# Performer attention and GEGLU on one core: one weighting of v moved to VectorE, and the stage between two tiles in another order

## The chip, the cores and the metric

The kernel runs on one core of one Trainium2 chip. The metric is the device time of one execution in microseconds (us). Most executions of one kernel agree within some tenths of a per cent: the 95% intervals of the ratios below reach 0.12 to 0.25% to each side, those of the three slow experiments (e10, e11, e13) up to 0.36%.

## The reference, cut to what matters

```python
q, k, v: (8 batches, 8 heads, 576, 64);  omega: (128, 64)
phi(x) = exp(x omega^T - |x|^2/2 - max) / sqrt(128)      # q and k scaled by 64^-1/4 first
kv  = phi(k)^T v ;  z = sum of phi(k)
num = phi(q) kv  ;  den = phi(q) z ;  attn = num / den
x   = attn as 4608 tokens x 512
out = (gelu(x w_gate) * (x w_val)) w_out                 # 512 -> 1536 -> 512
```

## The kernel before

The kernel interleaves the attention of one batch with the feed-forward of a tile of 512 tokens. It does not let a scheduler choose: every engine runs its instructions in the order in which the Python calls record them. So "an order" is a list of calls, and a change of order is a permutation of that list. The calls that the change and the argument touch:

```python
def fill(n):                    # n matmuls on zeros, results not used: work to keep TensorE going
    fill_ps = mo_tile([P, P], F32, "fill_ps")
    for _ in range(n):
        nc.tensor.matmul(fill_ps, still[:, :P], still[:, :P])

def load_v(b, eng=nc.gpsimd):   # 1152 KB, float32
    t = ld.tile([P, HP, R * D], F32, name="vf")
    loads.append(eng.dma_start(out=t, in_=rows_of(v, b)))

class Attention:                # a, n, m, o are batches 0, 1, 2, 3
    def by_dma(self, nm): ...   # k or q transposed by DMA, issued on SyncE's queue
    def kf(self, c, ...): ...   # TensorE: pk <- omegaT, kT
    def kx(self, c): ...        # ScalarE: k_p <- exp(pk)
    def km(self, c): ...        # VectorE: nmax <- max(pk)
    def qf / qx / w: ...        # pq; q_pT <- exp(pq); ScalarE: wk <- exp(nmax)
    def v(self, half, eng):     # v_ext <- v * wk, one half of the columns, 128x1152
        eng.tensor_mul(vev[:, isl, :, :D], vfv[:, isl], wkv[:, isl]...)
        eng.tensor_copy(vev[:, isl, :, D], wkv[:, isl])
    def kz / kzc: ...           # 72 matmuls of k_p with v_ext; copy of the result
    def nd / nx: ...            # q_pT with kz; x_sb <- num / den on VectorE
    def xd(self, i): ...        # nc.sync.dma_start_transpose: xT <- x_sb
    def xt / xc: ...            # the same by TensorE and a copy

    # feed-forward of a tile
    def ts(self, n, eng):       # x sum number n of four: difference of two parts of xT, 128x512
        eng.tensor_sub(t[:, n], p, q)       # two SBUF inputs; sum 1 reads sum 0
    def vm / vs / va: ...       # x w_val with 7 products in place of 8, out of w_val and the x sums
    def ga / gp / ge: ...       # x w_gate and gelu
```

In names, `val_one` and `val_two` are the products of `vm`, `g_ps` the gate, `o_ps` the projection of the tile before.

The softmax here doesn't subtract the row's maximum and nothing guards it: scores larger than these inputs give would overflow.

Of the kernel before, what the change touches and what calls it, by code (L numbers as in the profile page):

```python
# [15 lines left out]
def kernel(  # L16
# [11 lines left out]
    nc = tc.nc  # L28
# [40 lines left out]
    def mo_tile(shape, dtype, name):  # L69
        return mo.tile(shape, dtype, name=name, tag="mo")  # L70


    def rows_of(src, b):
        return src[b].rearrange("(j e) (p r) d -> (e p) j (r d)", e=2, r=R)
# [3 lines left out]
    def load_kq(nm, b, parts=1):  # L78
        src = {"k": k, "q": q}[nm]
        t = ld.tile([P, NI, P], BF16, name=f"{nm}_in")  # L80
        tv = t.rearrange("p i x -> p (i x)").rearrange("p (j y) -> p j y", j=HP)
        n = HP // parts
        loaded[nm, b] = t
        loads.extend(nc.gpsimd.dma_start(out=tv[:, c * n:(c + 1) * n],
                                         in_=rows_of(src, b)[:, c * n:(c + 1) * n])
                     for c in range(parts))
        return loads[-parts:]

    def load_v(b, eng=nc.gpsimd):
        t = ld.tile([P, HP, R * D], F32, name="vf")  # L90
        loaded["v", b] = t
        loads.append(eng.dma_start(out=t, in_=rows_of(v, b)))
        return loads[-1:]
# [37 lines left out]
    def fill(n):  # L131
# [3 lines that stand above are left out]
# [19 lines left out]
    act, dve, pool = nc.scalar.copy, nc.vector.tensor_copy, nc.gpsimd  # L154
# [425 lines left out]
    def after(dmas):  # L580

        behind(last["begun"], dmas)

    def behind(one, dmas):
        for dma in dmas:
            tc.add_manual_dep(dma.ins, one.ins.name, mybir.DependencyInfo(
                mybir.DependencyClass.Sync, mybir.DependencyReason.DATA))
# [5 lines left out]
    def first():  # L593
# [9 lines left out]
        a = Attention(0)  # L603
# [41 lines left out]
        a.qt.pe(0)  # L645
        fill(12)
        a.qf(1, True)
        a.v(1, pool)
        a.qt.copy(0, dve)
        a.v(0, nc.vector)  # L650
        fill(12)
# [6 lines left out]
        n = Attention(1)  # L658
# [4 lines left out]
        h = Gated(1)  # L663
# [112 lines left out]
        p = Projection(0, g)  # L776
# [3 lines left out]
        n.kx(1)  # L780
        n.km(1)
        m = Attention(2)
        behind(loads[-2], [m.by_dma("k")])
        m.by_dma("q")
        n.kt.pe(3)
# [20 lines left out]
        p.mm(0, 11, 12)  # L806
        n.km(2)
        n.w()
        p.oc(0, act)
        p.st(0)  # L810
        p.mm(2, 0, 3)
# [3 lines left out]
        m.kf(1, False)  # L815
        m.kx(1)
        p.mm(2, 6, 9)
        p.mm(3, 0, 3)
        m.kf(0, False)
        n.v(0, nc.vector)  # L820
        n.kz(0, True)
        m.km(1)
        m.qf(0, False)
        m.qx(0)
        m.km(0)
        n.v(1, pool)
        n.kz(1)
        m.kx(0)
        p.mm(3, 3, 6)
        p.mm(3, 6, 7)  # L830
        load_v(2, nc.sync)
        n.kzc(dve)
        n.nd(0, False)
        m.qf(1, True)
        m.qx(1)
        n.nd(1, False)
        p.mm(2, 9, 10)
        n.nx(0)
        n.nx(1)
        p.mm(2, 10, 12)  # L840
        n.xd(0)
        n.nd(2, False)
        p.oc(2, act)
        fill(12)
        n.nd(3, True)
        m.qf(2, False)
        n.xd(1)
        n.nx(2)
        n.xd(2)
        n.nx(3)  # L850
        m.kf(2, False)
        m.km(2)
        fill(12)
        n.xt(3)
        n.xc(3, dve)
        m.kf(3, True)
        m.km(3)
        m.qx(2)
        h.ts(0, nc.gpsimd)
        m.tails(False)  # L860
        m.qx(4)
        m.km(4)
        p.mm(3, 7, 10)
        h.ga(0, 0)
        m.kx(2)
        p.mm(3, 10, 12)
        o = Attention(3)
        n.nd(4, False)
        m.kx(3)
        m.w()  # L870
        p.oc(3, act)
        n.nx(4)
        h.ga(0, 1)
        after(load_kq("k", 3) + load_kq("q", 3) + load_v(3))
        m.qf(3, True)
        h.ts(2, nc.vector)
        m.qx(3)
        h.vm(0, 1)
        h.vs(0, 1, act)
        m.kx(4)  # L880
        h.vm(0, 5)
        h.ts(1, nc.vector)
        m.v(1, nc.vector)
        m.v(0, nc.vector)
        h.ga(6, 0)
        h.vm(0, 6)
        h.ga(6, 1)
        h.ts(3, nc.vector)
        h.vs(0, 6, act)
        p.st(3)  # L890
        h.vs(0, 5, act)
        h.vm(0, 7)
        h.va(0, 2)
        h.vm(0, 2)
        h.gp(7, 0, 2)
        h.gp(7, 2, 4)
        h.vm(0, 3)
        h.va(0, 1)
        h.vm(0, 4)
        h.va(0, 0)  # L900
        h.ge(6)
        m.kz(0, False)
        m.kz(1)
        m.kzc(dve)
        h.vm(1, 1)
        h.vm(1, 5)
        h.vm(1, 2)
        h.vs(1, 1, act)
        h.high(0, 0, nc.vector)
        h.ge(0)  # L910
        m.nd(0, False)
        h.vs(1, 5, dve)
        h.ge(7)
        h.vm(1, 6)
        h.vs(1, 6, act)
        p.st(2)
        h.high(0, 1, nc.vector)
        h.gp(1, 0, 2)
        h.gp(1, 2, 3)
        h.gp(1, 3, 4)  # L920
        h.ge(1)
        n.xd(4)
        m.nx(0)
        m.xd(0)
        h.vm(1, 3)
        h.vm(1, 7)
        h.va(1, 0)
        h.va(1, 1)
        h.va(1, 2)
        h.gp(2, 0, 2)  # L930
        m.nd(1, False)
        m.nx(1)
        h.low(1, nc.gpsimd)
        h.low(0, nc.gpsimd)
        h.vm(2, 1)
        h.vm(2, 5)
        h.vs(2, 1, act)
        o.by_dma("k")
        m.xd(1)
        h.vs(2, 5, dve)  # L940
        h.gp(3, 0, 2)
        h.vm(2, 6)
        h.high(1, 1, nc.gpsimd)
        h.gp(2, 2, 3)
        h.vs(2, 6, act)
        h.vm(1, 4)
        h.high(1, 0, nc.vector)
        h.gp(2, 3, 4)
        h.vm(2, 2)
        h.ge(2)  # L950
        o.by_dma("q")
        h.vm(2, 7)
        h.va(2, 2)
        h.vm(2, 3)
        h.va(2, 1)
        m.nd(2, False)
        m.nx(2)
        h.va(2, 0)
        h.gp(8, 0, 2)
        h.gp(8, 2, 4)  # L960
        h.ge(8)
        h.vm(2, 4)
        h.vm(3, 1)
        h.vs(3, 1, dve)
        h.gp(3, 2, 3)
        h.vm(3, 5)
        m.nd(3, False)
        h.vs(3, 5, act)
        h.low(2, nc.vector)
        h.high(2, 0, nc.vector)  # L970
        h.gp(5, 0, 2)
        p.st(1)
        h.vm(3, 6)
        h.gp(3, 3, 4)
        h.vm(3, 3)
        m.nx(3)
        h.vs(3, 6, act)
        h.vm(3, 2)
        h.va(3, 0)
        h.vm(3, 7)  # L980
        h.va(3, 2)
        h.ge(3)
        h.va(3, 1)
        h.gp(9, 0, 2)
        h.gp(9, 2, 4)
        h.ge(9)
        h.high(3, 1, nc.gpsimd)
        m.nd(4, False)
        h.high(2, 1, nc.gpsimd)
        h.vm(4, 1)  # L990
        h.vm(4, 5)
        h.vm(4, 2)
        h.vs(4, 1, act)
        m.xd(2)
        m.nx(4)
        h.vm(3, 4)
        h.high(3, 0, nc.vector)
        h.vm(4, 6)
        h.gp(4, 0, 2)
        h.gp(4, 2, 3)  # L1000
        h.gp(4, 3, 4)
        h.vs(4, 6, act)
        h.vm(4, 7)
        h.ge(4)
        h.vs(4, 5, dve)
        h.vm(4, 3)
        h.va(4, 2)
        h.low(3, nc.gpsimd)
        h.vm(5, 1)
        h.vs(5, 1, act)  # L1010
        h.va(4, 1)
        h.vm(5, 5)
        h.vs(5, 5, act)
        h.gp(10, 0, 2)
        h.gp(10, 2, 4)
        h.va(4, 0)
        h.vm(5, 2)
        h.va(5, 0)
        h.ge(10)
        h.high(4, 1, nc.gpsimd)  # L1020
        h.vm(5, 6)
        h.low(4, nc.gpsimd)
        h.vm(4, 4)
        h.high(4, 0, nc.vector)
        h.gp(5, 2, 3)
        h.gp(5, 3, 4)
        h.vm(5, 3)
        h.vs(5, 6, act)
        h.vm(5, 7)
        h.va(5, 2)  # L1030
        h.gp(11, 0, 2)
        h.gp(11, 2, 4)
        h.va(5, 1)
        h.ge(5)
        h.ge(11)
        h.low(5, nc.vector)
        h.vm(5, 4)
        m.xd(3)
        h.high(5, 0, nc.vector)
        h.high(5, 1, nc.vector)  # L1040
        m.xd(4)
        return h, o
    def step(t, p, a, n):
# [453 lines left out]
    with tc.manual_schedule(engines={E.Activation, E.PE, E.DVE, E.SP, E.Pool}):  # L1497
        g, a = first()
        for t in range(2, N_TOK):
            p = Projection(t - 1, g)  # L1500
            if t + 1 < B:
                n = Attention(t + 2) if t + 2 < B else None
                g, a = step(t, p, a, n), n
            else:
                g = bare(t, p)
        end(Projection(N_TOK - 1, g))
# [30 lines left out]
```

## Time and profile before

| | before |
|---|---|
| time | 341.71 us (3 runs, 341.54 to 342.11) |
| span of the profiled run | 340.1 us, granted clock 0.996 |
| wk of batch 0 begins | 14.89 us |
| first nd of batch 0 | 20.34 us |
| first pk of batch 2 | 55.10 us |
| first nd of batch 2 | 74.71 us |
| first pk of the next tile's stage | 91.04 us |

In the lines of the profile PE is TensorE, PEld its weight loads, DVE is VectorE, ACT ScalarE, POOL GpSimd, SPq the queue on which SyncE issues transfers, and L134 is line 134 of the kernel. A line of a timeline gives the start in us, the length in us, engine, line, operation, out<-in with their sizes, the count, and in brackets how long the engine stood idle before and what ended that.

The prediction below shows most of the lines of this profile. One group it does not show turned out to decide the case. It is GpSimd's product of v with wk, and GpSimd's x sums, of the whole kernel before; the three numbers are minimum, median and maximum in ns, then come the first and the last start:

```profile
L271 POOL TENSOR_TENSOR v_ext<-vf,wk x12: 2145/2155/3322, 15.2 to 244.6; 128x1152 bf16<-128x1152 f32 x12
L455 POOL TENSOR_TENSOR x_sums<-xT,x_sums x10: 1142/1148/1154, 97.7 to 238.2; 128x512 bf16<-128x512 bf16 x10
```

The same product takes 2.15 us or 3.32 us on the same engine. The long ones are those at 15.20 and 54.50, where VectorE multiplies the other half of v at the same time.

### The profile page before, as it was taken

To read this page: it belongs to the slowest core of one execution; us is meant where nothing else is said; L and a number is where in the kernel's file an instruction comes from. 1 tells how busy PE (TensorE), PEld (TensorE's weight loads), DVE (VectorE), ACT (ScalarE), POOL (GpSimd) and SP (SyncE) were. 2 spreads that over 40 slices of the span, in tenths; PEclk is the share of its full clock that TensorE was granted. 3 is DMA by queue.
4 is the path that set the end of the run, shared out by engine and by line. 5 is a ranking of instruction groups with operands and counts; after the bars stand their busy time and mean duration, and the time that the engine had idled before them with its cause. 6 is when DMAs were issued, how large, how long until landed. Compare 5 with 4: busy or idle time off the path is not lost.

```text
span 340.1 us, 7996 instructions
## 1 busy us (share of the span) xinstructions
PE 328.1 (96%) x3118; PEld 206.9 (61%) x3159; DVE 229.5 (67%) x483; ACT 214.3 (63%) x434; POOL 149.5 (44%) x152
## 2 busy tenths in 40 slices
PE   8889999999999999999999999999999999999994
PEld 4566455666646664566447654665466786686683
DVE  2975389989773768375936674667457677796783
ACT  3895366774778558756875677658765446626650
POOL 8326014123496447744684559477968400000000
PEclk9999999999999999999999999999999999999998
DMA  8999999699999255945497529871413040014004
GB/s 161 276 206 207 206 265 177 155 163 221 196 144 328 53 102 87 328 92 108 58 319 120 112 28 287 170 106 33 94 33 62 10 104 22 1 28 97 2 0 124
DMA packets 66437, 44.95 MB, mean 132 GB/s; under 512 B 46688, under 2 KB 59232, under 8 KB 66400
## 3 DMA queue, kind: packets, MB, share of 16 engines
q0 software_dynamic: 14848, 22.12, 31.7%
q1 hardware_dynamic: 51088, 21.51, 31.0%
q10 hardware_dynamic: 464, 0.82, 0.7%
q8 instruction: 24, 0.39, 0.5%
q14 instruction: 13, 0.11, 0.1%
HBM read 37.78 MB, written 9.44 MB: 139 GB/s over the span
## 4 chain that ended last, share of the span: by engine, by line
PE 84%; DVE 7%; issue 2%; ACT 2%; DMA 2%; POOL 1%; SPq 0%; DVEq 0%
PE g_ps L433 20%; PE o_ps L559 18%; PE val_one L378 11%; PE val_two L378 9%; PE out_one L533 5%; PE out_two L533 3%; PE g_ps L425 3%; PE v_ps L462 3%; PE kz_ps L285 3%; PE pk L220 2%; PE nd L302 2%; DVE nmax L233 2%; PE pq L242 2%; DVE x_sb L314 2%; DVE val_c L387 1%
## 5 line engine op out<-in xcount | busy, mean ns | idle before, releaser
L433 PE MATMUL g_ps<-xT,w_gate_sb 128*128 128x512 bf16 x352 | 108.2, 379 | 0.5
L440 ACT ACTIVATE g_gelu<-g_ps 128x512 bf16<-128x512 f32 x108 | 63.6, 597 | 54.1 <-PE g_ps L433 26.5
L559 PE MATMUL o_ps<-w_out_sb,gated 128*128 128x512 bf16 x275 | 64.6, 380 | 1.1 <-issue 0.6
L480 POOL TENSOR_TENSOR gated<-g_gelu,val_c 128x512 bf16<-128x512 bf16 x29 | 33.7, 1162 | 53.1 <-DVE iden L313 26.7
L387 DVE TENSOR_TENSOR val_c<-val_one,val_c 128x256 f32<-128x256 f32 x48 | 20.4, 424 | 49.0 <-ACT g_gelu L440 40.0
L559 PEld LDWEIGHTS <-gated 128*128 128x128 bf16 x288 | 26.5, 98 | 33.5 <-issue 3.9
L378 PEld LDWEIGHTS <-w_val_sb 128*128 128x128 bf16 x384 | 36.5, 98 | 16.9 <-DVE val_c L387 1.2
L383 ACT COPY val_c<-val_one 128x256 f32<-128x256 f32 x95 | 35.2, 371 | 11.1 <-PE val_one L378 7.9
L378 PEld LDWEIGHTS <-val_sums 128*128 128x128 bf16 x288 | 27.3, 98 | 24.3 <-DVE x_sb L314 3.8
L433 PEld LDWEIGHTS <-w_gate_sb 128*128 128x128 bf16 x376 | 34.9, 98 | 11.2
L233 DVE TENSOR_REDUCE nmax<-pk 128x8 f32<-128x1024 f32 (+2 forms) x43 | 39.8, 970 | 2.6 <-PE pk L220 1.2
L249 ACT ACTIVATE q_pT<-pq 128x512 bf16<-128x512 f32 (+1 forms) x68 | 34.6, 600 | 10.3 <-PE pq L242 9.9
L228 ACT ACTIVATE k_p<-pk 128x1024 bf16<-128x1024 f32 (+2 forms) x43 | 33.0, 833 | 8.0 <-PE pk L220 6.4
L378 PE MATMUL val_one<-x_sums,w_val_sb 128*128 128x256 bf16 x192 | 36.6, 273 | 0.3 <-DVE val_c L387 0.3
L387 DVE TENSOR_TENSOR val_c<-val_two,val_c 128x256 f32<-128x256 f32 x96 | 36.1, 415 | 0.8 <-PE val_two L378 0.7
L271 POOL TENSOR_TENSOR v_ext<-vf,wk 128x1152 bf16<-128x1152 f32 x12 | 28.2, 2348 | 14.7 <-ACT wk L260 14.7
L484 POOL TENSOR_TENSOR gated<-g_gelu,val_c 128x256 bf16<-128x256 bf16 x34 | 24.1, 711 | 14.7 <-ACT g_gelu L440 14.7
L314 DVE TENSOR_TENSOR x_sb<-nd,iden 128x512 bf16<-128x512 f32 (+2 forms) x41 | 27.7, 677 | 1.4
L564 DVE COPY o_sb<-o_ps 128x512 f32<-128x512 f32 x20 | 13.7, 686 | 19.4 <-PE o_ps L559 14.9
L383 ACT COPY val_c<-val_two 128x256 f32<-128x256 f32 x45 | 16.8, 372 | 12.0 <-PE val_two L378 12.0
L484 DVE TENSOR_TENSOR gated<-g_gelu,val_one 128x256 bf16<-128x256 bf16 x48 | 20.0, 416 | 6.0 <-ACT g_gelu L440 5.7
L302 PEld LDWEIGHTS <-q_pT 128*128 128x128 bf16 (+1 forms) x320 | 14.5, 100 | 7.9 <-issue 3.6
(104 smaller groups left out, 492.4 us busy)
## 6 DMA issues: line engine op xcount, KB each, us to landing
out_dram<-o_sb SPq DMA_DIRECT2D x68, 128.0 KB, 3.4
vf<-in_v_dram POOLq DMA_DIRECT2D x7, 1152.0 KB, 13.1
q_in<-in_q_dram POOLq DMA_DIRECT2D x8, 576.0 KB, 10.0
k_in<-in_k_dram POOLq DMA_DIRECT2D x7, 576.0 KB, 6.8
w_gate_sb<-in_moe_w_gate_dram POOLq DMA_DIRECT2D x3, 512.0 KB, 18.1
w_val_sb<-in_moe_w_val_dram POOLq DMA_DIRECT2D x3, 512.0 KB, 19.6
w_out_sb<-in_moe_w_out_dram POOLq DMA_DIRECT2D x3, 512.0 KB, 13.2
vf<-in_v_dram SPq DMA_DIRECT2D x1, 1152.0 KB, 7.6
```

The lines of the kernel that those rows point to most:

```text
L228: last["begun"] = nc.scalar.activation(self.k_p[:, gs, i0:i0 + n, :], pk, func=Exp)
L233: nc.vector.reduce_max(self.nmax[:, gs, i0:i0 + n], pk, axis=AX, negate=True)
L249: last["begun"] = nc.scalar.activation(dst[:, a, i0:i0 + n], self.pq[c][a].rearrange("m (i e p) -> m i e p", e=2, p=SP), func=Exp)
L314: nc.vector.tensor_mul(x_sb[:n].rearrange("p (g h d) -> p g h d", g=2, h=4)[:, gs], ndv[:, :, :, :D], iden[:n, gs].broadcast_to((n, gs.sto ...
L378: nc.tensor.matmul(ps, w[:, c, self.i * P:(self.i + 1) * P], x[:, c], start=first and c == 0, stop=c == 1, skip_group_check=not first)
L383: copy(self.c[:, {1: 0, 6: 1, 5: 2}[n]], self.beta if n == 5 else self.one)
L387: nc.vector.tensor_add(part, (self.gamma, self.beta, self.one)[k], part)
L433: last["begun"] = nc.tensor.matmul(self.gps[jf], w_gate_sb[:, jm, jf * P:(jf + 1) * P], x_tiles[self.t][:, jm], start=(jm == 0), stop=(jm ...
L440: nc.scalar.activation(self.gelus[jf][:, part], src, func=Gelu)
L480: eng.tensor_mul(self.gated[:, i, :], self.gelus[i], self.v[i].row())
L484: eng.tensor_mul(self.gated[:, i + HF, ts], self.gelus[i + HF][:, ts], s.c[:, 2] if half else s.one)
L559: nc.tensor.matmul(self.ps[qq], self.g.gated[:, f, qq * P:(qq + 1) * P], w_out_sb[:, f, :], start=(jf == 0), stop=(jf == N_DFF - 1))
```

## The change

Its intent is to finish the weighting of v of batch 0 earlier, and to close the waits of TensorE between 47 and 92 us by another order of the projection of tile 1, the attention of batches 1 and 2 and the first pairs of tile 2. The core of the diff:

```diff
-        a.v(1, pool)
+        a.v(1, nc.vector)
         a.qt.copy(0, dve)
         a.v(0, nc.vector)
 ...
         m = Attention(2)
+        fill(12)
         behind(loads[-2], [m.by_dma("k")])
         m.by_dma("q")
 ...
         n.w()
+        n.v(1, pool)
+        fill(12)
+        load_v(2, nc.sync)
 ...
         p.oc(2, act)
-        fill(12)
 ...
         m.km(2)
-        fill(12)
         n.xt(3)
-        n.xc(3, dve)
+        n.xc(3, act)
 ...
+        m.w()
+        m.v(0, nc.vector)
+        h.ts(0, nc.gpsimd)
+        h.ts(1, nc.gpsimd)
 ...
-        h.ts(1, nc.vector)
-        m.v(1, nc.vector)
-        m.v(0, nc.vector)
 ...
-        m.kzc(dve)
+        m.kzc(act)
 ...   (some 100 further calls moved, some fifteen copies, sums and products given to another engine)
```

More of the change, by code (lines that the diff above doesn't have):

```diff
@@ L817, in first @@
         p.mm(2, 6, 9)
+        p.mm(2, 9, 10)
         p.mm(3, 0, 3)
@@ L823, in first @@
         m.qf(0, False)
+        n.kz(1)
         m.qx(0)
         m.km(0)
-        n.v(1, pool)
-        n.kz(1)
+        n.kzc(dve)
+        n.nd(0, False)
+        n.nx(0)
         m.kx(0)
+        m.qf(1, True)
+        n.nd(1, False)
+        n.nx(1)
+        p.mm(2, 10, 12)
+        m.qx(1)
+        n.nd(2, False)
+        n.nx(2)
         p.mm(3, 3, 6)
         p.mm(3, 6, 7)
-        load_v(2, nc.sync)
-        n.kzc(dve)
-        n.nd(0, False)
-        m.qf(1, True)
-        m.qx(1)
-        n.nd(1, False)
@@ L837, in first @@
-        p.mm(2, 9, 10)
-        n.nx(0)
-        n.nx(1)
-        p.mm(2, 10, 12)
-        n.xd(0)
-        n.nd(2, False)
-        p.oc(2, act)
-        fill(12)
-        n.nd(3, True)
-        m.qf(2, False)
-        n.xd(1)
-        n.nx(2)
-        n.xd(2)
-        n.nx(3)
+        n.xd(0)
+        n.xd(1)
+        n.nd(3, True)
+        n.nx(3)
+        m.qf(2, False)
+        n.xd(2)
+        p.oc(2, act)
+        m.qx(2)
+        p.st(2)
         m.kf(2, False)
         m.km(2)
-        fill(12)
@@ L854, in first @@
         n.xt(3)
-        n.xc(3, dve)
+        n.xc(3, act)
+        o = Attention(3)
         m.kf(3, True)
         m.km(3)
-        m.qx(2)
-        h.ts(0, nc.gpsimd)
         m.tails(False)
         m.qx(4)
+        m.kx(2)
+        p.mm(3, 7, 10)
+        p.mm(3, 10, 12)
+        p.oc(3, act)
+        p.st(3)
         m.km(4)
-        p.mm(3, 7, 10)
+        m.kx(4)
         h.ga(0, 0)
-        m.kx(2)
-        p.mm(3, 10, 12)
-        o = Attention(3)
+        h.ga(0, 1)
         n.nd(4, False)
+        n.nx(4)
@@ L869, in first @@
+        m.w()
+        m.v(0, nc.vector)
+        h.ts(0, nc.gpsimd)
+        h.ts(1, nc.gpsimd)
+        h.vm(0, 1)
+        h.vm(0, 5)
         m.kx(3)
-        m.w()
-        p.oc(3, act)
-        n.nx(4)
-        h.ga(0, 1)
+        h.vm(0, 2)
         after(load_kq("k", 3) + load_kq("q", 3) + load_v(3))
-        m.qf(3, True)
-        h.ts(2, nc.vector)
+        h.vs(0, 1, act)
+        h.vs(0, 5, act)
+        h.ga(6, 0)
+        m.qf(3, False)
         m.qx(3)
-        h.vm(0, 1)
-        h.vs(0, 1, act)
@@ L880, in first @@
-        m.kx(4)
-        h.vm(0, 5)
-        h.ts(1, nc.vector)
-        m.v(1, nc.vector)
-        m.v(0, nc.vector)
-        h.ga(6, 0)
+        h.ga(6, 1)
+        n.xd(4)
         h.vm(0, 6)
-        h.ga(6, 1)
-        h.ts(3, nc.vector)
         h.vs(0, 6, act)
-        p.st(3)
-        h.vs(0, 5, act)
-        h.vm(0, 7)
-        h.va(0, 2)
-        h.vm(0, 2)
         h.gp(7, 0, 2)
         h.gp(7, 2, 4)
+        h.ts(3, nc.vector)
+        h.ge(0)
+        h.ts(2, nc.vector)
+        m.v(1, nc.vector)
@@ L897, in first @@
+        h.vm(0, 7)
+        h.ge(6)
+        h.va(0, 2)
         h.vm(0, 3)
         h.va(0, 1)
+        m.kz(0, False)
+        m.kz(1)
+        m.kzc(act)
+        h.high(0, 1, nc.gpsimd)
         h.vm(0, 4)
         h.va(0, 0)
-        h.ge(6)
-        m.kz(0, False)
-        m.kz(1)
-        m.kzc(dve)
         h.vm(1, 1)
+        h.vs(1, 1, act)
+        h.high(0, 0, nc.vector)
         h.vm(1, 5)
         h.vm(1, 2)
-        h.vs(1, 1, act)
-        h.high(0, 0, nc.vector)
-        h.ge(0)
+        h.low(0, nc.gpsimd)
@@ L911, in first @@
+        h.va(1, 0)
         m.nd(0, False)
-        h.vs(1, 5, dve)
-        h.ge(7)
-        h.vm(1, 6)
-        h.vs(1, 6, act)
-        p.st(2)
-        h.high(0, 1, nc.vector)
+        o.by_dma("k")
         h.gp(1, 0, 2)
         h.gp(1, 2, 3)
+        m.nx(0)
+        h.gp(2, 0, 2)
+        h.vm(1, 6)
+        h.vs(1, 5, act)
+        h.vm(1, 3)
+        h.vs(1, 6, dve)
+        h.va(1, 1)
+        h.ge(7)
         h.gp(1, 3, 4)
         h.ge(1)
-        n.xd(4)
-        m.nx(0)
-        m.xd(0)
@@ L925, in first @@
-        h.vm(1, 3)
-        h.vm(1, 7)
-        h.va(1, 0)
-        h.va(1, 1)
-        h.va(1, 2)
-        h.gp(2, 0, 2)
+        h.low(1, nc.gpsimd)
         m.nd(1, False)
         m.nx(1)
-        h.low(1, nc.gpsimd)
-        h.low(0, nc.gpsimd)
+        o.by_dma("q")
         h.vm(2, 1)
+        h.vs(2, 1, act)
+        h.vm(1, 7)
+        h.va(1, 2)
+        h.gp(2, 2, 3)
+        h.high(1, 1, nc.vector)
+        m.xd(0)
+        h.gp(2, 3, 4)
+        h.ge(2)
         h.vm(2, 5)
-        h.vs(2, 1, act)
@@ L938, in first @@
-        o.by_dma("k")
-        m.xd(1)
-        h.vs(2, 5, dve)
+        h.vs(2, 5, act)
         h.gp(3, 0, 2)
         h.vm(2, 6)
-        h.high(1, 1, nc.gpsimd)
-        h.gp(2, 2, 3)
-        h.vs(2, 6, act)
         h.vm(1, 4)
         h.high(1, 0, nc.vector)
-        h.gp(2, 3, 4)
+        m.nd(2, False)
+        m.nx(2)
+        h.vs(2, 6, act)
         h.vm(2, 2)
-        h.ge(2)
-        o.by_dma("q")
         h.vm(2, 7)
@@ L954, in first @@
         h.vm(2, 3)
-        h.va(2, 1)
-        m.nd(2, False)
-        m.nx(2)
-        h.va(2, 0)
         h.gp(8, 0, 2)
         h.gp(8, 2, 4)
+        h.va(2, 1)
+        h.va(2, 0)
+        h.gp(3, 2, 3)
         h.ge(8)
-        h.vm(2, 4)
+        h.high(2, 1, nc.gpsimd)
         h.vm(3, 1)
         h.vs(3, 1, dve)
-        h.gp(3, 2, 3)
+        h.vm(2, 4)
         h.vm(3, 5)
         m.nd(3, False)
-        h.vs(3, 5, act)
-        h.low(2, nc.vector)
         h.high(2, 0, nc.vector)
+        h.vs(3, 5, dve)
         h.gp(5, 0, 2)
-        p.st(1)
         h.vm(3, 6)
+        h.vs(3, 6, dve)
+        m.nx(3)
         h.gp(3, 3, 4)
+        h.vm(3, 2)
         h.vm(3, 3)
-        m.nx(3)
-        h.vs(3, 6, act)
-        h.vm(3, 2)
+        h.va(3, 1)
+        h.low(2, nc.gpsimd)
+        m.xd(1)
+        h.gp(9, 0, 2)
+        h.ge(3)
+        h.gp(9, 2, 4)
+        h.ge(9)
         h.va(3, 0)
@@ L981, in first @@
         h.va(3, 2)
-        h.ge(3)
-        h.va(3, 1)
-        h.gp(9, 0, 2)
-        h.gp(9, 2, 4)
-        h.ge(9)
         h.high(3, 1, nc.gpsimd)
         m.nd(4, False)
-        h.high(2, 1, nc.gpsimd)
+        m.nx(4)
         h.vm(4, 1)
+        h.vs(4, 1, act)
         h.vm(4, 5)
         h.vm(4, 2)
-        h.vs(4, 1, act)
-        m.xd(2)
-        m.nx(4)
+        h.vs(4, 5, dve)
         h.vm(3, 4)
-        h.high(3, 0, nc.vector)
         h.vm(4, 6)
+        h.va(4, 0)
+        h.vs(4, 6, act)
         h.gp(4, 0, 2)
@@ L1001, in first @@
         h.gp(4, 3, 4)
-        h.vs(4, 6, act)
+        h.ge(4)
+        h.high(3, 0, nc.vector)
         h.vm(4, 7)
-        h.ge(4)
-        h.vs(4, 5, dve)
         h.vm(4, 3)
-        h.va(4, 2)
+        h.va(4, 1)
         h.low(3, nc.gpsimd)
         h.vm(5, 1)
-        h.vs(5, 1, act)
-        h.va(4, 1)
+        h.vs(5, 1, dve)
         h.vm(5, 5)
@@ L1015, in first @@
         h.gp(10, 2, 4)
-        h.va(4, 0)
+        h.ge(10)
+        h.va(4, 2)
+        h.high(4, 1, nc.vector)
+        h.vm(5, 6)
         h.vm(5, 2)
-        h.va(5, 0)
-        h.ge(10)
-        h.high(4, 1, nc.gpsimd)
-        h.vm(5, 6)
         h.low(4, nc.gpsimd)
@@ L1027, in first @@
         h.vm(5, 3)
+        m.xd(2)
         h.vs(5, 6, act)
@@ L1032, in first @@
         h.gp(11, 2, 4)
+        p.st(1)
         h.va(5, 1)
@@ L1035, in first @@
         h.ge(11)
+        h.va(5, 0)
         h.low(5, nc.vector)
@@ L1039, in first @@
         h.high(5, 0, nc.vector)
-        h.high(5, 1, nc.vector)
+        h.high(5, 1, nc.gpsimd)
         m.xd(4)
```

## The prediction

> **What bounds the kernel now.** I read the page's busy line and its chain first, then the chain in order of time around 14 to 30 us, then the timeline of each engine from 47 to 92 us, because the diff touches only these two stretches.
>
> ```profile
> PE 328.1 (96%) x3118; PEld 206.9 (61%) x3159; DVE 229.5 (67%) x483; ACT 214.3 (63%) x434; POOL 149.5 (44%) x152
> PE 84%; DVE 7%; issue 2%; ACT 2%; DMA 2%; POOL 1%; SPq 0%; DVEq 0%
> ```
>
> TensorE bounds the whole, but other engines own the chain for 14% of the span, and that is where an order can gain. First the start (columns: start us, length us, what):
>
> ```profile
> 14.89 0.24 ACT wk L260
> 15.20 3.32 POOL v_ext L271
> 18.52 0.22 POOL v_ext L273
> 18.79 0.77 PE kz_ps L285 x36
> 19.59 0.71 DVE kz L291
> ```
>
> The weighting of v of batch 0 has two halves; GpSimd's half (3.32 us) ends last and releases the second half of the kz matmuls. VectorE's half is short, and a copy ran on VectorE while wk was being made:
>
> ```profile
> 14.77 0.41 DVE L181 COPY qT<-qT_ps 128x512 bf16<-128x512 bf16 x1
> 15.15 1.36 DVE L271 TENSOR_TENSOR v_ext<-vf,wk 128x1152 bf16<-128x1152 f32 x1
> 16.43 0.23 DVE L273 CAST v_ext<-wk 128x18 bf16<-128x18 f32 x1
> ```
>
> Then the searched stretch. Four chain lines give TensorE's pace (512 columns: 4 in 0.86, so 0.2167 each). From 47.14 to 72.58 it has 48 output matmuls (10.4), 12 gate matmuls' worth (2.6), 7 pairs of value matmuls of 256 columns (1.5), the score matmuls of batches 1 and 2 (pk 1.7, pq 1.0), 72 kz (1.2), 40 nd (1.3), 24 fills (1.3) and transposes (0.5): 21.5 us of work in 25.4 us, so **3.9 us of holes**. From 72.58 to 91.04 I count 35 value pairs (7.6), 36 gate matmuls (7.8), 72 kz (1.3) and 40 nd (1.3): 17.9 in 18.5, **0.5 us of holes**. The holes are caused by VectorE and ScalarE (start, length, engine, operation, idle before it):
>
> ```profile
> 51.12 4.05 PE L559 MATMUL o_ps<-w_out_sb,gated 128*128 128x512 bf16 x18 [0.16 <-issue]
> 55.10 0.40 PE L220 MATMUL pk<-omegaT,kT 64*128 64x128 bf16 x8
> ...
> 61.49 0.83 PE L134 MATMUL fill_ps<-still 128*128 128x128 bf16 x12
> 62.16 0.41 PE L302 MATMUL nd<-kz,q_pT 128*128 128x65 bf16 x8
> ```
>
> ```profile
> 55.54 1.02 ACT L228 ACTIVATE k_p<-pk 128x1024 bf16<-128x1024 f32 x1 [0.15 <-PE pk L220]
> ```
>
> ```profile
> 56.60 2.36 DVE L233 TENSOR_REDUCE nmax<-pk 128x8 f32<-128x1024 f32 x2 [0.65 <-ACT k_p L228]
> ```
>
> ```profile
> 57.00:63.00 6.00, 5.78 (x144) 4.33 (x139) 5.39 (x12) 3.69 (x7) 1.02 (x2) 1.00 0.95 248
> 63.00:69.00 6.00, 5.57 (x65) 3.47 (x61) 5.89 (x14) 5.16 (x12) 1.91 (x3) 1.00 0.30 45
> 69.00:75.00 6.00, 5.52 (x108) 3.84 (x106) 4.92 (x11) 4.09 (x9) 1.49 (x2) 1.00 0.99 171
> ```
>
> In the windows the sums are PE, PEld, DVE, ACT, POOL: VectorE is busy 5.39 and 5.89 of 6 us, so it, not TensorE, sets the pace from about 57 to 69 us. Up to 55 us TensorE is dense: 18 matmuls at 0.2167 are 3.9 of the 4.05.
>
> **What the Trainium skill says.** "Perfetto Trace Analysis", Identifying the Most-Contended Engine: matmul busy share misjudges the headroom. Agreed: the page gives a gate matmul 379 ns, yet they start 217 ns apart, so I counted work by pace. "GPSIMD Engine Reference", Engine selection: two-input elementwise work is about twice as slow there. Here the same 128x1152 product took 3.32 against 1.36 us, 2.4 times. "PSUM — Partial Sum Buffer", PSUM bank collisions: two engines must not touch one bank at a time, so programs order them. The trace agrees: the maximum at 56.60 waited 0.65 us for the exponential that reads the same tile. "TensorE: Matmul & The Clock Gate", What's actually happening: after about 3.4 us without work the clock halves. Fills guard against that; the longest wait in TensorE's list is 1.2 us and the granted clock is 1.00 in all windows above, so no drop is seen.
>
> **Part A, v of batch 0 on VectorE.** The second half is now ahead of the qT copy in VectorE's order, and the first half behind it. With start-to-start distances from the rows: wk is ready at 15.15; product 1.28, cast 0.15, copy 0.33, product 1.28, cast 0.23, end at 18.42. GpSimd ended at 18.73. So v is complete 0.31 earlier. But the first 36 kz matmuls (0.58 by their pace), which ran at 17.65 while GpSimd still worked, need the half that is now last. They fall behind the wait: 0.58 - 0.31 = **+0.27 us**. From 27 to 47 us TensorE is dense, so this should stay. The load of k for batch 2 can be issued 3 us sooner, but the DMA share is 1.2 there and the loads ahead of it are not moved; I count nothing.
>
> **Part B, the searched order.** Instruction counts stay, except who does some. The two runs of 12 fills (0.67 us each) leave 61.49 and 63.10, where the next nd and transposes were waiting for ScalarE and VectorE anyway (free), and go to about 47.4 and 54.5, where TensorE is dense (paid). Walking the order by the rows' durations, in the clock of the kernel before:
> - Fill one delays the last score tiles of batch 1, hence their maxima on VectorE, by 0.6. Fill two and one more gap bring the first score tile of batch 2 from 55.10 to 56.5, its exponential to 56.9, the maximum behind it from 56.60 to about 57.95: **+1.35**.
> - From there VectorE works without a long wait: two maxima 2.3, kz copies 0.7, wait for nd 0.45, three normalisations at 0.84, a split one 1.1, maxima 1.15 + 1.2 + 0.6: the last maximum of batch 2 ends at 68.0, against 67.1 before. The lag falls to +0.9, because xt's copies (2 x 0.4) went to ScalarE; later an x sum (0.34) goes to GpSimd and the kz copy (0.62) to ScalarE.
> - Then ScalarE is the chain: exponential 0.55, wk 0.15, exponentials 1.05, value copies 0.54, q exponentials 1.05, value copy 0.3, table load 1.28, two gelus 1.05, kz copy 0.65: 74.6. The first nd of batch 2 needs that copy; it stood at 74.71 with the same TensorE work done ahead of it. So **-0.1**: the fills cost 1.35 early and the shorter VectorE queue gives it back.
> - In the rest the holes are 0.5; I take **-0.2**.
>
> The sum is +0.27 - 0.1 - 0.2 = about 0. The walk has some 60 hops of which each can be 0.02 to 0.05 off, so it is good to about 1 us. One choice is not from a row: somebody searched this order and kept it, so I lean 0.4 us to the fast side. **341.3 us.**
>
> **Rivals.**
> 1. The holes close: if VectorE's lag of 1.35 does not arise (because fill one falls into a wait I don't see), the same walk ends 1.3 earlier, near 340. For it: 3.9 us of holes. Against it: 18 matmuls in 4.05 us around the new places.
> 2. ScalarE becomes the bound from 68 to 75 (my walk leaves it no gap) and its table load delays the kz copy further, or GpSimd's x sums (1.15 each) and the later load of k, q and v of batch 3 (after 69.8, not 68.2) come late for tile 2: 342.5 to 343. Against it: the transpose of k started at 77.82 before and the load lands in 6.8, so near 77.5 still.
> 3. Without fills at 61 to 64 the clock drops: some 3 us at half pace, 344 or more. Against it: no hole in my walk is over 1 us.
>
> **Range and chances.** Rivals 1 and 2 span 340 to 343; I take 339.7 to 343.0. 2% is 6.8 us, more than all holes of both stretches (4.4) could give: faster 0.015. Slower needs rival 3 or a missed stall: 0.015.
>
> **What would show it.** A right: the kz matmuls run in one piece from about 18.5 and nd starts near 20.6, not 20.34. B right: the first pk of batch 2 near 56.8 (with A's shift), the last maximum of batch 2 near 68.3, the first nd of batch 2 near 74.9, the next tile's pk at 91.0 within 0.6. Wrong if TensorE has waited at the fills' new places, if the granted clock falls below 1 between 55 and 75, or if stages after 92 change in length; I expect them equal within 0.3 us.

## The result

| | median | lowest to highest | runs |
|---|---|---|---|
| before, same rounds | 341.62 us | 341.19 to 342.11 | 4 |
| after | 342.50 us | 342.31 to 342.90 | 4 |

The ratio is 1.0027, with a 95% interval of 1.0009 to 1.0044. A ratio is the mean time of one kernel's runs over that of the other's of the same rounds, so it is not quite the ratio of the medians. The change costs 0.9 us; by the 2% rule that is "same". It lies inside the predicted range and on the other side of zero from the predicted number.

The page of after, its busy line and the shares of its chain:

```profile
PE 329.4 (97%) x3159; PEld 206.1 (61%) x3159; DVE 229.7 (67%) x482; ACT 214.5 (63%) x435; POOL 150.3 (44%) x152
PE 89%; DVE 5%; ACT 1%; POOL 1%; DMA 1%; issue 0%; SPq 0%; POOLq 0%
```

TensorE owns more of the chain than before (89% against 84%), and the kernel is slower. So a larger share of the engine that bounds the kernel is no proof of fewer holes. Why it rose by five points was not looked into; the 24 fills, 1.3 us or 0.4% of the span, are too small for it, and the page of before shows 3118 matmuls to 3159 weight loads, so some records are missing.

**First the offset.** All positions of after must be shifted before they are compared. The first fills of the two kernels, in the timeline of TensorE, before and then after:

```profile
5.22 1.25 PE L134 MATMUL fill_ps<-still 128*128 128x128 bf16 x10
```

```profile
5.16 0.73 PE L134 MATMUL fill_ps<-still 128*128 128x128 bf16 x10
```

Up to here the two programs are the same, yet these ten matmuls took 1.25 and 0.73 us. Runs of the other kernels show 0.73, 0.91 to 0.93 or 1.25, whatever was changed later. By this and other small differences everything behind is up to 0.8 us early or late by chance (wk of batch 0 begins between 14.15 and 14.93 in the fourteen traces; in e7 below at 14.75, though its fills took 0.73). I therefore measure part A from wk of batch 0, and part B from the first nd of batch 0 (20.34 before, 19.87 after).

**Part A.** TensorE's and VectorE's timelines of after:

```profile
14.41 1.36 DVE L271 TENSOR_TENSOR v_ext<-vf,wk 128x1152 bf16<-128x1152 f32 x1 [0.30 <-ACT wk L260]
...
16.10 1.35 DVE L271 TENSOR_TENSOR v_ext<-vf,wk 128x1152 bf16<-128x1152 f32 x1
17.37 0.23 DVE L273 CAST v_ext<-wk 128x18 bf16<-128x18 f32 x1
```

```profile
17.74 1.34 PE L285 MATMUL kz_ps<-v_ext,k_p 64*128 64x65 bf16 x72 [0.25 <-DVE v_ext L273]
...
19.87 0.40 PE L302 MATMUL nd<-kz,q_pT 128*128 128x65 bf16 x8 [0.24 <-DVE kz L291]
```

The 72 kz matmuls run in one piece behind the wait. From wk (14.15) to nd it is 5.72 us, against 5.45 before: +0.27.

**Part B.** Positions after the first nd of batch 0, each read from the timelines:

| | before | after | difference |
|---|---|---|---|
| first pk of batch 2 | 34.76 | 36.10 | +1.34 |
| end of the last maximum of batch 2 | 46.78 | 47.72 | +0.94 |
| first nd of batch 2 | 54.37 | 55.21 | +0.84 |
| first pk of the next tile's stage | 70.70 | 71.58 | +0.88 |
| from there to the end | 249.06 | 248.95 | -0.11 |

The fills' cost arrives as predicted (+1.34), and VectorE's shorter queue takes 0.4 of it back as predicted. The hop that was to take the rest back, from the last maximum to nd, does not. The first nd of batch 2, before and then after:

```profile
74.71 0.40 PE L302 MATMUL nd<-kz,q_pT 128*128 128x65 bf16 x8
```

```profile
75.08 0.41 PE L302 MATMUL nd<-kz,q_pT 128*128 128x65 bf16 x8
```

The timelines of after show what stands in front of it: TensorE's with the fills at their new places, then GpSimd's, VectorE's and TensorE's again:

```profile
47.00 0.84 PE L134 MATMUL fill_ps<-still 128*128 128x128 bf16 x12
...
53.91 0.83 PE L134 MATMUL fill_ps<-still 128*128 128x128 bf16 x12
...
55.97 0.40 PE L220 MATMUL pk<-omegaT,kT 64*128 64x128 bf16 x8
```

```profile
67.17 1.15 POOL L455 TENSOR_TENSOR x_sums<-xT 128x512 bf16<-128x512 bf16 x1 [8.95 <-ACT k_p L228]
68.40 2.85 POOL L455 TENSOR_TENSOR x_sums<-xT,x_sums 128x512 bf16<-128x512 bf16 x1
```

```profile
68.90 1.34 DVE L271 TENSOR_TENSOR v_ext<-vf,wk 128x1152 bf16<-128x1152 f32 x1
```

```profile
71.31 0.38 PE L378 MATMUL val_one<-x_sums,val_sums 128*128 128x256 bf16 x2 [0.96 <-POOL x_sums L455]
```

GpSimd's second x sum takes 2.85 us, though its like takes 1.15 everywhere else in both kernels. It runs from 68.40 to 71.25, and VectorE multiplies v from 68.90 to 70.24. TensorE waits 0.96 us for that sum, and in TensorE's list of waits from 66 to 76 us it is the only one. The granted clock there is 1.00 (the row gives the window, its length, the busy us of PE, PEld, DVE, ACT and POOL, then the granted clock, the DMA share and GB/s):

```profile
69.00:75.00 6.00, 5.04 (x100) 3.52 (x99) 4.79 (x10) 5.18 (x11) 4.94 (x5) 1.00 0.64 104
```

"SBUF — State Buffer", Who interferes with whom, in the Trainium skill, has a sentence for this pair: "A DVE instruction with two SBUF inputs contends with a GpSimd instruction that reads SBUF". v's product and the x sum both read two SBUF tiles, so the theory was ready to be tested.

### The profile page after: what moved, and what is told of

It reads as the page before. It is cut to its first block, busy times and chain, and to the rows that moved or that the text cites. A ratio compares the mean times of both kernels' runs of the same rounds, so it can differ in the third digit from the quotient of the medians.

```text
span 340.4 us, 8042 instructions
## 1 busy us (share of the span) xinstructions
PE 329.4 (97%) x3159; PEld 206.1 (61%) x3159; DVE 229.7 (67%) x482; ACT 214.5 (63%) x435; POOL 150.3 (44%) x152
## 4 chain that ended last, share of the span: by engine, by line
PE 89%; DVE 5%; ACT 1%; POOL 1%; DMA 1%; issue 0%; SPq 0%; POOLq 0%
PE g_ps L433 24%; PE o_ps L559 18%; PE val_one L378 13%; PE val_two L378 9%; PE out_one L533 5%; PE out_two L533 3%; PE g_ps L425 3%; PE v_ps L462 3%; PE nd L302 3%; PE kz_ps L285 3%; PE pk L220 2%; DVE nmax L233 2%; PE pq L242 2%; POOL x_sums L455 1%; DMA omega_f<-in_omega_dram 1%; DVE x_sb L314 1%
## 5 line engine op out<-in xcount | busy, mean ns | idle before, releaser
L433 PE MATMUL g_ps<-xT,w_gate_sb 128*128 128x512 bf16 x376 | 113.2, 379 | 0.0
L559 PE MATMUL o_ps<-w_out_sb,gated 128*128 128x512 bf16 x288 | 65.9, 380 | 0.0
L480 POOL TENSOR_TENSOR gated<-g_gelu,val_c 128x512 bf16<-128x512 bf16 x30 | 34.8, 1161 | 48.0 <-DVE iden L313 26.3
L383 ACT COPY val_c<-val_one 128x256 f32<-128x256 f32 x92 | 34.1, 371 | 8.5 <-PE val_one L378 5.5
L271 POOL TENSOR_TENSOR v_ext<-vf,wk 128x1152 bf16<-128x1152 f32 x11 | 24.9, 2259 | 11.6 <-ACT wk L260 11.6
```

Of the source, the lines that this page charges most:

```text
L383: copy(self.c[:, {1: 0, 6: 1, 5: 2}[n]], self.beta if n == 5 else self.one)
L433: last["begun"] = nc.tensor.matmul(self.gps[jf], w_gate_sb[:, jm, jf * P:(jf + 1) * P], x_tiles[self.t][:, jm], start=(jm == 0), stop=(jm ...
L480: eng.tensor_mul(self.gated[:, i, :], self.gelus[i], self.v[i].row())
L559: nc.tensor.matmul(self.ps[qq], self.g.gated[:, f, qq * P:(qq + 1) * P], w_out_sb[:, f, :], start=(jf == 0), stop=(jf == N_DFF - 1))
```

## The experiments

**Theory:** part B carries the loss. It has two sources: fills that are now paid, and the x sum stretched by VectorE's product. **Rivals:** part A carries it; the engine change of the x sum alone carries it (GpSimd is simply slower); the clock; a late transfer.

All ratios are to the kernel before. Positions are in us after the first nd of batch 0, "wk to nd" apart.

| run | ratio (95%) | median us | before, same rounds | wk to nd | pk of batch 2 | nd of batch 2 | next tile's pk |
|---|---|---|---|---|---|---|---|
| before | | | | 5.45 | 34.76 | 54.37 | 70.70 |
| after | 1.0027 (1.0009 to 1.0044) | 342.50 | 341.62 | 5.72 | 36.10 | 55.21 | 71.58 |
| e1, A alone | 0.9991 (0.9978 to 1.0003) | 341.39 | 341.69 | 5.72 | 35.19 | 54.57 | 70.90 |
| e6, A alone again | 0.9989 (0.9965 to 1.0014) | 341.71 | 341.93 | 5.72 | 35.24 | 54.83 | 71.16 |
| e2, B alone | 1.0034 (1.0020 to 1.0047) | 342.81 | 341.69 | 5.45 | 36.10 | 55.22 | 71.58 |
| e3, second x sum on VectorE | 1.0010 (0.9998 to 1.0023) | 342.07 | 341.69 | 5.72 | 36.11 | 54.50 | 70.86 |
| e4, v's product later | 1.0010 (0.9997 to 1.0024) | 342.13 | 341.69 | 5.71 | 36.11 | 54.87 | 71.24 |
| e5, after without fills | 0.9995 (0.9971 to 1.0020) | 342.01 | 341.93 | 5.72 | 35.09 | 55.12 | 71.48 |
| e7, before without fills | 0.9987 (0.9961 to 1.0013) | 341.74 | 341.93 | 5.45 | 35.05 | 54.62 | 70.95 |
| e8, e5 and e3 together | 0.9970 (0.9946 to 0.9994) | 341.13 | 341.93 | 5.71 | 34.77 | 53.89 | 70.26 |
| e12, e8 with A undone | 0.9982 (0.9969 to 0.9994) | 341.37 | 341.96 | 5.45 | 34.99 | 54.29 | 70.66 |
| e11, e5 and v loaded early | 1.0117 (1.0081 to 1.0152) | 346.23 | 341.96 | 5.72 | 34.79 | 60.90 | 77.26 |
| e10, e8 and v loaded early | 1.0135 (1.0105 to 1.0166) | 347.17 | 341.96 | 5.71 | 34.77 | 61.50 | 77.86 |
| e13, before and v loaded early | 1.0157 (1.0122 to 1.0192) | 347.71 | 341.96 | 5.44 | 34.83 | 61.24 | 77.57 |

All twelve gave correct results.

### Which part carries the loss: e1, e6 and e2

e1 is the kernel before with A alone:

```diff
-        a.v(1, pool)
+        a.v(1, nc.vector)
```

> The kernel before with part A alone: all of v of batch 0 on VectorE, nothing reordered. My step A: kz in one piece, nd of batch 0 later by 0.27 us after wk, and 0.27 us longer in all, so a ratio near 1.0008. Rival (freeing GpSimd early lets loads land sooner and wins that back): 1.000 or below. By the trace, nd starts 5.72 us after wk (in the kernel before 5.45).

e2 is the changed kernel with that line turned back.

> The changed kernel with part A undone: half of v of batch 0 back on GpSimd. If the two parts add up, it is 0.27 us shorter than the changed kernel, so 0.6 us longer than the kernel before (ratio 1.0018). If part A carries the loss, the ratio is 1.000.

e2 has the whole loss (1.0034), and its trace equals that of after at the three positions of the table, to 0.01 us. So B carries it. It did not get 0.27 us shorter than after, as I had expected: its median is 0.3 us longer, with overlapping intervals. e1's trace shows A's +0.27 at its place, but its times show no loss. I repeated it:

> The kernel before with part A alone (v of batch 0 all on VectorE), a repeat of the first run of this edit, whose interval (0.9978 to 1.0003) just excluded what its trace showed. By the trace, nd of batch 0 comes 0.27 us later after wk and this carries on: ratio 1.0008. By the first timed run: 0.999. If this run is near 1.000 the two together say that A is worth nothing that times can show.

The trace gave 5.72 again, the times 0.9989. What becomes of A's 0.27 is open: nine of nine traces with A have it (5.71 or 5.72), five of five without have 5.44 or 5.45, and the intervals of the two timed runs reach from 0.35% faster to 0.14% slower. In before and e1, e6, e7, the first pk of batch 2 comes anywhere from 34.76 to 35.24, with a wait for k's transposition (0.40 in e1 and e6) or for ScalarE in front of it, so the few tenths of A go under in that. What lies behind varies as much: from the first pk of the next tile's stage to the end it is 248.5 us in e1 and 249.3 in e2, with all other traces between.

### The stretched x sum: e3 and e4

e3 gives the second x sum to VectorE, ahead of v's product; e4 leaves it on GpSimd and moves v's product behind the other x sums.

```diff
e3:                                    e4:
-        m.v(0, nc.vector)             -        m.v(0, nc.vector)
         h.ts(0, nc.gpsimd)                     h.ts(0, nc.gpsimd)
-        h.ts(1, nc.gpsimd)                     h.ts(1, nc.gpsimd)
+        h.ts(1, nc.vector)             ...
+        m.v(0, nc.vector)                      h.ts(2, nc.vector)
                                       +        m.v(0, nc.vector)
                                                m.v(1, nc.vector)
```

> The changed kernel with the second x sum on VectorE ahead of v instead of on GpSimd. Theory (GpSimd's second x sum, stretched from 1.15 to 2.85 us by VectorE's product of v, holds TensorE 0.96 us): TensorE's wait goes, the first nd of batch 2 comes about 0.8 us sooner, ratio to the kernel before 1.0003. Rival (ScalarE's queue and table load hold that nd anyway): the wait moves to ScalarE's kz copy, gain below 0.3 us, ratio about 1.002.

> The changed kernel with the first half of v of batch 2 put behind the two x sums of VectorE, just ahead of the second half; both GpSimd sums stay. Theory (the two engines stretch GpSimd only while VectorE multiplies two arrays in SBUF): GpSimd's second x sum falls from 2.85 to about 1.2 us, TensorE's wait on it goes, the gain is 0.6 us (kz then waits for v), ratio 1.0009. Rival (2.85 us is what that sum costs behind the first one, whatever VectorE does): it stays above 2.5 us and the time gets no better than the changed kernel.

e4 is the cleaner test. Same operation, same engine, same place, only the company is gone (GpSimd's timeline, then TensorE's):

```profile
68.68 1.15 POOL L455 TENSOR_TENSOR x_sums<-xT,x_sums 128x512 bf16<-128x512 bf16 x1
```

```profile
73.44 0.76 PE L285 MATMUL kz_ps<-v_ext,k_p 64*128 64x65 bf16 x36 [0.59 <-DVE v_ext L273]
```

The sum takes 1.15 instead of 2.85 us, so the stretch comes from VectorE's product, and the rival "GpSimd is simply slower" falls. The two kernels hold a control that needs no edit: GpSimd's product `gated<-g_gelu,val_c` of 128x512 keeps its 1.16 to 1.18 us with VectorE's `gated<-g_gelu,val_one` in its midst (before at 108.23, 113.22, 117.01 and more), where one of VectorE's two inputs, val_one, lies in PSUM. Beside VectorE's `gated<-g_gelu,val_c`, with both inputs in SBUF (before at 127.16), GpSimd's 128x256 product takes 0.93 us in place of 0.67. But v is then late, and kz waits 0.59 us: of the gain 0.34 is left at nd. In e3 no wait takes its place, and nd of batch 2 comes 0.71 earlier. Both intervals now hold 1.000. By e3's trace this source is 0.7 of the 0.9 us, by its times somewhat over half (1.0010 in place of 1.0027, from two chip sessions).

### The fills: e5 and e7

```diff
e5 (after):                            e7 (before):
         m = Attention(2)                       p.oc(2, act)
-        fill(12)                      -        fill(12)
 ...                                    ...
         n.v(1, pool)                           m.km(2)
-        fill(12)                      -        fill(12)
```

> The changed kernel without its two runs of 12 fills. Theory (fills are paid at their new places, nothing else needs them): the first pk of batch 2 comes about 1.3 us earlier relative to wk than in the changed kernel (41.8 us after wk there, so about 40.5), and of that 1.0 to 1.3 us reach the end: 341.2 to 341.5, ratio to the kernel before about 0.999. The stretching of GpSimd's second x sum by VectorE's product of v stays (2.8 us, TensorE waits about 1 us for it). Rival one, fills absorbed in a wait that the walk did not see: first pk of batch 2 moves by under 0.3 us and the time stays at 342.5. Rival two, the clock needs the fills: granted clock under 1.00 between 55 and 75 us and 343 us or more.

> The kernel before without its two runs of 12 fills in the same stage (61.49 and 63.10 us there). Theory (they filled a wait for ScalarE and VectorE): no change within 0.3 us, ratio 0.999 to 1.001, and the wait appears in front of the nd and transposes that followed them. Rival, they were paid there too: 1.3 us shorter, ratio 0.996. Rival, they kept the clock up: granted clock under 1.00 at 61 to 69 us and a longer time.

e7 confirms that the fills were free where they stood: 0.9987 with 1 inside the interval, no gain at the next tile (70.95), and a wait in their place (TensorE's timeline of e7):

```profile
62.91 0.40 PE L220 MATMUL pk<-omegaT,kT 64*128 64x128 bf16 x8 [0.45 <-DVE x_sb L314]
```

The clock did not need them: granted 1.00 in the windows from 57 to 75 us of e5 and e7. That ends the rival of the clock for waits of this length, up to 0.7 us.

e5 is a miss of my expectation. The first pk of batch 2 came 1.01 earlier, VectorE kept this up to the end of its last maximum (46.71, 1.01 earlier), and at nd of batch 2 only 0.09 was left in the trace. The next rows of e5's TensorE and GpSimd show where it went:

```profile
67.42 0.60 PE L425 MATMUL g_ps<-xT,w_gate_sb 128*128 128x256 bf16 x4 [0.69 <-DMA xT<-x_sb]
...
71.67 0.38 PE L378 MATMUL val_one<-x_sums,val_sums 128*128 128x256 bf16 x2 [1.03 <-POOL x_sums L455]
```

```profile
67.54 1.15 POOL L455 TENSOR_TENSOR x_sums<-xT 128x512 bf16<-128x512 bf16 x1 [9.52 <-DMA xT<-x_sb]
68.77 2.85 POOL L455 TENSOR_TENSOR x_sums<-xT,x_sums 128x512 bf16<-128x512 bf16 x1
```

The x sums wait for the DMA transpositions of x, whose end came only 0.1 us earlier, and the second sum is stretched still. One row per kernel says why: the first transposition of x on SyncE's queue, in e5 and then in after.

```profile
L322 SPq DMA_TRANSPOSE xT<-x_sb x1: 2110/2110/2110, 61.4 to 61.4; - x1
```

```profile
L322 SPq DMA_TRANSPOSE xT<-x_sb x1: 1199/1199/1199, 61.9 to 61.9; - x1
```

It took 2.11 us to issue in e5 and 1.20 in after. In e5 the load of v of batch 2 was issued on the same queue at 55.80 and landed 6.3 us later, at 62.1, so it was still in flight; in after it was issued at 54.71, landed 6.4 later at 61.1, and the transposition began at 61.92. In the four kernels with fills at the new places (after, e2, e3, e4) all x transpositions took 1.2; in before, e1, e6, e7, e5 and e8, without them, one of three took 1.66 to 2.11. So the paid fills hid a second limit that lies close behind them.

The times of e5 (0.9995) are better than its trace: its six runs go from 341.34 to 342.55, and the profiled one is the slowest. The trace is one draw, and fills are worth something between 0.1 us (trace) and 1.1 us (ratio to before, against that of after, from two chip sessions). In the rounds of e5 to e8 the kernel before scattered more than in the others: two of its eleven runs took 343.44 and 343.77 us. Without these two the ratios of e5, e6, e7 and e8 would be 1.0006, 1.0000, 1.0000 and 0.9981, and the upper figure for the fills 0.7 us.

### Both together: e8

e8 is e5 with e3's edit.

> The changed kernel without the two runs of fills and with the second x sum on VectorE ahead of the product of v. If the two losses (fills 1.0 to 1.3 us, stretched x sum 0.4 by its timed run or 0.7 by its trace) are separate and add: 340.4 to 341.1, ratio to the kernel before 0.996 to 0.998, which would beat both kernels. If they are one slack seen twice (TensorE waits for whichever comes last): about 341.4, no better than without fills alone.

e8 beats the kernel before, by 0.9970 with the interval below 1 (each of its six runs, up to 341.51, lies below the median of before, 341.93), and so also the changed kernel, with which it was not run in the same rounds. At nd of batch 2 it is 1.32 earlier than after. That splits into 0.59 from the fills (seen at the last nd of batch 1, just ahead of the x sums) and 0.73 from the x sum (the wait of 0.96 is gone). The gain is larger than e3's 0.71 and e5's 0.09 together, because of the fills' share e5 had kept only 0.09 at that same place. e8's first pk of batch 2 came 0.32 earlier than e5's, with no wait in front of it, and its long transposition took 1.95 where e5's took 2.11; together that is the difference of 0.5. Neither is an effect of the x sum, which comes later, so I take it for the spread of these transfers from run to run. TensorE still waits 0.62 us for the transposition in e8.

### The load in front of the transposition: e11, e10 and e13

```diff
         behind(loads[-2], [m.by_dma("k")])
+        load_v(2, nc.sync)
         m.by_dma("q")
 ...
-        load_v(2, nc.sync)
```

> The changed kernel without its fills, and with the load of v of batch 2 (1.15 MB, 6.3 us to land) issued ahead of the transposition of q instead of behind it. Without fills alone, the first pk of batch 2 came 1.01 us earlier than in the changed kernel (counted from the first nd of batch 0), and at the first nd of batch 2 only 0.09 was left; the first x transposition by DMA took 2.11 us to issue instead of 1.20 while that load was in flight. Theory (the load's tail stretches the transposition): with the load some 3 us earlier all x transpositions take 1.2, GpSimd's first x sum starts about 0.8 us earlier (at 46.4 after that nd, not 47.2) and so does the first nd of batch 2 (54.3, not 55.1): 341.2, ratio to the kernel before 0.998. Rival (the transposition's length has nothing to do with the load): 2.1 again and no change from without fills alone. Risk for both: the transposition of q now runs beside the load and comes late for the first pq of batch 2.

> Changed kernel without fills, second x sum on VectorE, and v of batch 2 loaded ahead of the transposition of q. Without the last edit TensorE waited 0.62 us for the DMA transposition of x (1.95 us issue of the first). Theory: that wait goes, the next tile's pk comes 0.3 to 0.6 earlier than 70.26 after the first nd of batch 0, and the ratio to the kernel before is about 0.996. Rival: no change from 0.997.

> The kernel before with v of batch 2 loaded ahead of the transposition of q instead of after the first score stages. There one of the three x transpositions took 1.96 us while the load was in flight. Theory: all three take 1.2, GpSimd's first x sum starts about 0.7 us earlier; the end gains at most 0.3, for TensorE waited only 0.3 us for that transposition and ScalarE and VectorE own the chain behind it. Rival: the transposition stays at 1.9.

All three lost 1.2 to 1.6%, by the risk that e11's expectation had named and not sized. SyncE's queue in e11, then in after:

```profile
51.64 0.57 SPq L92 DMA_DIRECT2D vf<-in_v_dram  x1
52.32 8.71 SPq L170 DMA_TRANSPOSE qT<-q_in  x1
```

```profile
51.90 2.76 SPq L170 DMA_TRANSPOSE qT<-q_in  x1
54.71 0.57 SPq L92 DMA_DIRECT2D vf<-in_v_dram  x1
```

And TensorE in e11, at the first matmul that needs it:

```profile
63.13 0.61 PE L242 MATMUL pq<-qT,omegaT 64*128 64x512 bf16 x2 [5.54 <-DMA qT<-q_in]
```

The transposition of q, issued behind the load, held the queue 8.71 us; in e10 and e13 it was 8.90 and 8.38. It ended at 61.03, and the load landed at 61.04 (51.64 and 9.4). TensorE waited 5.5 us for it. That wait cost the granted clock too: it was 1.00 from 55 to 61 us and 0.50 from 63 to 69, where the same pq took 0.61 in place of 0.39 us.

```profile
63.00:69.00 6.00, 5.03 (x67) 3.25 (x69) 2.98 (x8) 3.67 (x6) 0.00 (x0) 0.50 0.22 51
```

In e10 it was 0.50 as well, in e13 0.71. So the loss is the wait and a slow stretch behind it. The six runs of e11 fit that: the one with a mean clock of 0.996 took 343.72 us, those with 0.990 took 345.7 to 347.9. How the loss divides was not measured.

The x transpositions, now with no load in flight, took 1.20 to 1.22 in all three. So the runs show both sides, the transposition behind the load that got longer and those without a load that got shorter, and they show that this place for the load is the wrong one. They do not show that the queue is the reason. In the kernel before, k of batch 3 is transposed while loads issued on GpSimd's queue are in flight, and it takes just as long (SyncE's queue):

```profile
77.82 7.18 SPq L170 DMA_TRANSPOSE kT<-k_in  x1
```

It ended at 85.00, and the load of v of batch 3, issued at 69.71, landed 15.3 later, at 85.0; in after the same pair is 83.27 and 83.3. In these traces the long transpositions of k and q end within 0.1 us of the landing of v, whichever queue it was issued on. "DMA: Bandwidth & Descriptors", Queues, rings and completion order, in the Trainium skill, says that SP's transfers share one row of rings and that each engine takes descriptors in ring order. This order fits e11, but not k's transposition of batch 3, for which the load was on another queue. What it does not give either is why in before the first x transposition (61.06, 1.22 us) passed while that load was in flight and the second (62.4, 1.96 us) did not. That stays open.

### A undone on the best one: e12

> The same without the load's move, and with part A undone (v of batch 0 split between GpSimd and VectorE again). Trace: first nd of batch 0 at 5.45 after wk instead of 5.71 (0.27 earlier), carried on to the end: ratio to the kernel before about 0.9962. If the timed runs of A alone (0.999 twice) were right against their traces, A undone costs 0.3 us: 0.998.

e12 (0.9982) has nd of batch 0 0.27 earlier after wk and yet ends no earlier than e8 (0.9970); the intervals overlap. Its number is that of the second expectation. Its transposition took 2.11 us where e8's took 1.95. Which of the two forms of A is better can't be told from these runs.

## Why the prediction was right or wrong

The range and the class held. The central number was 1.2 us short, and the direction was wrong.

- **Step A, +0.27 us:** right in the trace to 0.01, in every trace with the edit. Not visible in times.
- **Fills free before, paid after:** right. +1.35 was predicted at the first pk of batch 2, +1.34 measured; e7 shows them free at the old places.
- **Lag of +0.9 at the last maximum:** right, +0.94.
- **"So -0.1: the fills cost 1.35 early and the shorter VectorE queue gives it back":** this is the step that failed. The walk let ScalarE own 68 to 74.6 us and found no other wait. Measured is +0.84. The missing term is the second x sum: I entered GpSimd's sums with 1.15 us each, and it took 2.85. By e3, where nothing else differs, this term is worth 0.71 us at nd. The rest, about 0.2 us, is the size of the walk's own error.
- **"In the rest ... I take -0.2":** measured +0.04 from nd to the next tile's pk.
- **The lean of 0.4 to the fast side** had no row behind it, and the experiments show that the order kept by the search was beaten by two edits of it.
- **Rival 1** did not come. **Rival 2** came in part: GpSimd's x sums did come late, for a reason that it didn't name. The loads of batch 3 harmed nothing: k's transposition starts at 76.94, before at 77.82. **Rival 3** is refuted by e5 and e7; a drop of the clock is seen only in e10, e11 and e13, behind waits of 5.4 to 5.5 us.

The evidence for the missing term lay in the profile before. I had quoted 3.32 against 1.36 us and called it the ratio of the two engines. The group's minimum of 2.15 says that 1.17 of the 3.32 was contention.

## What to carry to other kernels

When one operation of one shape has two durations on the same engine, find what ran beside the long one before using either number, and do not put a product with two SBUF inputs on VectorE beside a GpSimd sum that TensorE waits for. A fill is free only where its engine waits for something later than the fill; when an order moves, fills have to be looked at again, and removing one may only uncover the next limit. Before a transposition by DMA, look at what loads are still in flight, on its own queue or another. And a long wait of TensorE can cost twice: behind the one of 5.5 us the clock was at half.

## What the Trainium skill lacked or had wrong

- "SBUF — State Buffer", Who interferes with whom, says that issue order decides which of the two engines is blocked. The traces agree where VectorE comes second: in before its x sum at 68.01, begun inside GpSimd's (67.09 to 68.24), took 0.51 instead of 0.42 us. In after GpSimd's sum is recorded as the first to begin (68.40, VectorE's product 68.90), and yet VectorE took its usual 1.34 us and GpSimd was stretched from 1.15 to 2.85. It ended 1.01 us behind the product, so nearly all of its own 1.15 us came after it; the same holds for the stretched products of v. Whether the rule fails here or GpSimd's record begins before it first reads can't be told from these runs; the page does not say how such a start is to be read.
- "GPSIMD Engine Reference", Engine selection, gives about a factor of two for elementwise work. Uncontended, the 128x1152 product took 2.15 against 1.36 us (1.6 times), and the 128x512 bfloat16 sum 1.15 against 0.42 us (2.7 times).
- "DMA: Bandwidth & Descriptors" has no figure for a DMA transposition of SBUF data beside a large load in flight. Here q's held the queue for 8.4 to 8.9 us in place of 2.7 to 3.5, behind a load of 1152 KB on the same queue, and k's took 6.3 to 7.2 us, with loads of GpSimd's queue in flight.
